# Attention in one core of Trainium2: six score tiles in one run, then all the values, with a marker read between the two key halves

## The chip, the cores and the metric

One core of one Trainium2 chip runs the whole program. The metric is the device time of one execution in microseconds (us), a median over runs. The core has five engines that work side by side, each through its own list of instructions in order: PE (TensorE, matrix multiplication; PEld is its weight load), DVE (VectorE), ACT (ScalarE), POOL (GpSimd) and SP (SyncE). POOL and SP here mostly issue DMA transfers. An engine that reaches an instruction whose input is not there waits, and everything behind it in its list waits too. Results of PE land in PSUM, which has eight banks per partition; one bank holds 512 numbers of 32 bits.

## The reference

Sigmoid attention over 8 batches, 12 heads, 448 positions and head size 64, then a feed-forward layer with an exact GELU. The program spends its first quarter in the attention and the rest in the feed-forward layer.

```python
# q, k, v: (8, 12, 448, 64); w_in: (768, 2048); w_out: (2048, 768)
scores = (1.0 / np.sqrt(64)) * np.matmul(q, k.transpose(0, 1, 3, 2)) - np.log(448)
attn = 1.0 / (1.0 + np.exp(-scores))
y = np.matmul(attn, v)
x = y.transpose(0, 2, 1, 3).reshape(8 * 448, 12 * 64)
h = x @ w_in
out = (0.5 * h * (1.0 + erf(h / np.sqrt(2)))) @ w_out
```

## The kernel before

**Units.** The attention works in 24 units. Unit u is one batch and two pairs of heads, p = 0 and 1, with two heads j = 0 and 1 in each pair. The 448 keys of a head are three full chunks of 128 (c = 0, 1, 2) and a tail of 64. Scores are computed with the keys as output rows and the 448 queries as columns.

**Scores.** `scores(u, p, c)` makes one score tile for a pair: two heads, so two banks. The head size is 64, so a matmul needs only half of the rows of PE's array: head j takes row half j, and the two heads run side by side (64 rows by 128 columns each, "64*128" in the profile). For accuracy each of q and k is split in a high and a low part (`split_qk`, tiles `hi` and `lo`, 128x896 each), and three products are added, so a tile is three pairs of matmuls. Unit 0 has plain operands of 32 bits. The tail of all four heads is one tile, `scores_tail(u)`, made from the raw q and k with quarters of the array ("64*64"). After each tile ACT makes the probabilities `a` with a sigmoid (L353).

**Values.** The products with v have an output of 64 rows. For units 1 to 21, `quarters(u, turn)` uses four quarters of the array at a time (both pairs, both heads, one half of a chunk's 128 keys). In turn 0 pair p takes key half p, in turn 1 the other. Both turns add into the same two banks, so turn 1 may not run beside turn 0. `values_tail(u)` adds the 64 tail keys the same way. Units 0, 22 and 23 ("plain") use `values` with all 128 rows instead.

**Order.** The order of each engine's instructions is the order of the code: it is written out by hand (`manual_schedule`), and a wait is put only where data or a buffer asks for it. In a pass u of the main loop PE does the first three score tiles of unit u, turn 0 and the tail values of unit u-1, the other three score tiles and the tail scores of unit u, and turn 1 of unit u-1. So the scores run one unit ahead of the values, and PE goes back and forth between 64*128 and 64*64 twice in a pass.

**The other engines in a pass.** ACT has seven sigmoids, for units 3 to 17 the high part of pair 0 of the next unit (L342), and two steps of the weight decoder (L132, L135). DVE copies the two finished banks of unit u-1 to the tile `x` (`park`, L452), runs the decoder's `start` (L121, L122, L125) and `end` (L141, L146), and makes the splits (L344, L345). The decoder turns 64-bit weights into 32-bit ones; its chunks 0 to 15 are 128x768, the rest 128x512. `decode(u, place)` takes so many of its steps (start, scale, end) at three places in a pass. POOL then stores `x` to `scr_x` (L455) and decoded weights to `scr_f`. There is one buffer for `x`, so the next `park` waits until the store has landed. SP loads q, k, v and the raw weights.

**PSUM.** Three buffers of two banks for score tiles (`ps_sc`), one bank each for pair 0 and pair 1 of the values (`ps_av`). The feed-forward layer takes all eight banks after the attention.

**The end.** The feed-forward layer starts with two operand tiles `xh0`, `xl0` that were loaded and split during units 16 to 20; the next two (`xl`, split on L288 and L289) are loaded by SP when the attention's memory is free.

Of the kernel before, what the change touches and what calls it, by code (L numbers as in the profile page):

```python
# [16 lines left out]
P = 128  # L17
# [4 lines left out]
def tile_sigmoid_attention_gelu_ffn(  # L22
# [34 lines left out]
    one = const.tile([P, 8], F32, name="one")[:, :1]  # L57
# [147 lines left out]
    STEPS = {B * NU - 2: (2, 1, 1), B * NU - 1: (3, 2, 2)}  # L205
# [98 lines left out]
    x0 = []  # L304

    def attention(at, ps_sc, ps_av):
# [3 lines left out]
        def load(u):  # L310
# [4 lines left out]
            for ps in (slice(0, 1), slice(1, 2)) if u == 0 else (slice(0, 2),):  # L315
                hps = slice(2 * n + ps.start, 2 * n + ps.stop)
                nc.sync.dma_start(raw[:, ps, 0], q[b, hps].rearrange("p r s -> r p s"))
                for j in range(2):
                    src = k[b, hps, rows(j), j].rearrange("p r s -> r p s")
                    queue = nc.scalar if j == 0 and u == 0 else nc.sync  # L320
                    queue.dma_start(raw[rows(j), ps, 1], src)
# [59 lines left out]
        def scores_tail(u):  # L381
# [3 lines left out]
            sc = ps_sc.tile([P, 2, 512], F32, tag="sc", name=f"sc{u}_t")[:, :, :S]  # L385
# [10 lines left out]
        def bank(u, p):  # L396
            if (u, p) not in pavs:
                pavs[u, p] = ps_av.tile([P, 512], F32, tag=f"pav{p}", name=f"pav{u}_{p}")
            return pavs[u, p][:, :S]

        def values(u, p, chunks=range(FULL)):
            if u < 0:
                return
            pav = bank(u, p)
            for c in chunks:
                a = probs.pop((u, p, c))
                for j in range(2):
                    nc.tensor.matmul(  # L408
                        pav[rows(j)],
                        vals[u][:, p, j, c],  # L410
                        a[:, j],
                        start=c == 0 and (p == 0 or u == total - 1),
                        stop=c == FULL - 1 and p == 1 and u < total - 1,
                    )

        def values_tail(u):
            if u < 0:
                return
            a = probs.pop((u, 0, FULL))
            for p, j in QUARTERS:  # L420
                nc.tensor.matmul(  # L421
                    bank(u, p)[rows(j)],
                    vals[u][rows(p), p, j, FULL],
                    a[rows(p), j],
# [482 lines left out]
```

## Time and profile before

| | us |
|---|---|
| median of 3 runs | 1033.49 (1033.11 to 1035.11) |
| the profiled execution, its own time | 1033.18 |
| its span in the trace | 1031.4 |
| first score matmul, in the chain that ended last | 5.11 |
| first matmul of the feed-forward layer, there | 250.46 |
| PE busy in the span | 1026.4 |
| DVE busy, ACT busy | 783.4, 605.2 |

The profiled execution took 1.8 us more than its span, which lies around the span. The rows below are from that one execution. In a row of the time line the columns are: start in us, length in us, engine, line of the code, operation, output<-input, shape, how many were merged, and in brackets how long the engine had been idle and what ended that. PE's matmuls overlap each other, so the distance between two starts says what one costs, not its length.

### The profile page before, as it was taken

To read this page: it belongs to the slowest core of one execution; us is meant where nothing else is said; L and a number is where in the kernel's file an instruction comes from. 1 tells how busy PE (TensorE), PEld (TensorE's weight loads), DVE (VectorE), ACT (ScalarE), POOL (GpSimd) and SP (SyncE) were. 2 spreads that over 40 slices of the span, in tenths; PEclk is the share of its full clock that TensorE was granted. 3 is DMA by queue.
4 is the path that set the end of the run, shared out by engine and by line. 5 is a ranking of instruction groups with operands and counts; after the bars stand their busy time and mean duration, and the time that the engine had idled before them with its cause. 6 is when DMAs were issued, how large, how long until landed. Compare 5 with 4: busy or idle time off the path is not lost.

```text
span 1031.4 us, 16513 instructions
## 1 busy us (share of the span) xinstructions
PE 1026.4 (100%) x6429; PEld 908.1 (88%) x6429; DVE 783.4 (76%) x989; ACT 605.2 (59%) x804; POOL 118.0 (11%) x186
## 2 busy tenths in 40 slices
PE   9999999999999999999999999999999999999998
PEld 5555555556999999999999999999999999999998
DVE  3676767795799688997678888566888875678875
ACT  6788787875445465455366645644665555466552
POOL 0111112001323362115000000100000000000000
PEclk9999999999999999999999999999999999999999
DMA  9999999995688798588644445734444553434441
GB/s 300 310 305 308 296 314 297 330 306 183 214 265 265 259 318 314 154 287 308 201 148 123 127 132 163 236 98 136 136 122 125 161 167 101 123 109 137 137 135 66
DMA packets 85933, 211.84 MB, mean 205 GB/s; under 512 B 9376, under 2 KB 35872, under 8 KB 85856
## 3 DMA queue, kind: packets, MB, share of 16 engines
q1 hardware_dynamic: 70672, 155.20, 50.2%
q0 software_dynamic: 14880, 55.26, 15.0%
q8 instruction: 50, 0.82, 0.3%
q10 hardware_dynamic: 304, 0.34, 0.1%
q14 instruction: 27, 0.22, 0.1%
HBM read 163.38 MB, written 50.33 MB: 207 GB/s over the span
## 4 chain that ended last, share of the span: by engine, by line
PE 100%; DVE 0%; DVEq 0%; issue 0%
PE pf L545 75%; PE pav L436 10%; PE sc L370 9%; PE sc_t L387 2%; PE pav L421 2%; PE pav L408 1%; PE warm L468 0%; DVE zero L464 0%; DVE tmp L582 0%; DVEq L903 0%; DVE one L465 0%
## 5 line engine op out<-in xcount | busy, mean ns | idle before, releaser
L545 PE MATMUL pf<-op,whl 128*128 128x448 f32 x2016 | 382.8, 353 | 0.0
L545 PEld LDWEIGHTS pf<-op,whl 128*128 128x128 f32 x2016 | 380.3, 189 | 1.8 <-DVE op L582 0.8
L253 ACT CAST whl<-wst 128x768 fp32r<-128x768 f32 x212 | 176.4, 833 | 241.5 <-PE pf L545 212.7
L545 PE MATMUL pf<-xh_p,whl 128*128 128x448 f32 x1008 | 273.4, 352 | 0.0
L260 DVE TENSOR_TENSOR whl<-wst,whl 128x768 fp32r<-128x768 f32 x212 | 201.8, 953 | 51.7 <-ACT whl L253 51.6
L545 PEld LDWEIGHTS pf<-xh_p,whl 128*128 128x128 f32 x1008 | 190.5, 189 | 0.2
L545 PE MATMUL pf<-xl_p,whl 128*128 128x448 f32 x504 | 177.6, 352 | 0.0
L353 ACT ACTIVATE a<-sc 128x896 f32<-128x896 f32 x144 | 121.2, 916 | 42.5 <-PE sc L370 42.5
L582 DVE TENSOR_TENSOR op<-g,op 128x896 fp32r<-128x896 f32 x112 | 121.4, 1085 | 1.4 <-ACT op L592 1.3
L592 ACT CAST op<-g 128x896 fp32r<-128x896 f32 x112 | 104.7, 935 | 2.6 <-PE pf L545 2.6
L545 PE MATMUL pf<-xh,whl 128*128 128x448 f32 x384 | 104.3, 353 | 0.0
L436 PE MATMUL pav<-a,v 64*64 64x448 f32 x1008 | 103.7, 540 | 0.0
L545 PEld LDWEIGHTS pf<-xl_p,whl 128*128 128x128 f32 x504 | 95.3, 189 | 0.0
L436 PEld LDWEIGHTS pav<-a,v 64*64 64x64 f32 x1008 | 36.7, 133 | 52.6 <-issue 47.6
L545 PEld LDWEIGHTS pf<-xh,whl 128*128 128x128 f32 x384 | 72.6, 189 | 0.7 <-issue 0.7
L582 DVE TENSOR_TENSOR g<-g,g 128x896 f32<-128x896 f32 x64 | 69.4, 1084 | 0.0
L452 DVE COPY x<-pav 128x448 f32<-128x448 f32 x48 | 27.9, 620 | 52.9 <-PE pav L436 44.2
L545 PE MATMUL pf<-xl,whl 128*128 128x448 f32 x192 | 67.7, 352 | 0.0
L579 ACT ACTIVATE g<-tmp 128x448 f32<-128x448 f32 x72 | 45.2, 627 | 36.1 <-DVE tmp L582 36.1
L582 DVE TENSOR_TENSOR tmp<-pf,g 128x448 f32<-128x448 f32 x72 | 44.9, 624 | 27.1 <-PE pf L545 26.6
L582 DVE TENSOR_TENSOR g<-pf,g 128x448 f32<-128x448 f32 x48 | 29.9, 624 | 33.8 <-PE pf L545 33.8
L370 PEld LDWEIGHTS sc<-lo,hi 64*128 64x128 f32 x276 | 26.0, 185 | 32.9 <-ACT a L353 18.1
(80 smaller groups left out, 975.1 us busy)
## 6 DMA issues: line engine op xcount, KB each, us to landing
wst<-scr_out SPq DMA_DIRECT2D x112, 384.0 KB, 3.2
wst<-scr_in SPq DMA_DIRECT2D x84, 384.0 KB, 3.1
v<-v_dram SPq DMA_DIRECT2D x24, 512.0 KB, 6.7
raw<-w_in_dram SPq DMA_DIRECT2D x16, 768.0 KB, 6.2
raw<-w_out_dram SPq DMA_DIRECT2D x24, 512.0 KB, 5.3
scr_x<-x POOLq DMA_DIRECT2D x24, 448.0 KB, 6.6
out_dram<-tmp SPq DMA_DIRECT2D x47, 224.0 KB, 2.2
qk<-q_dram SPq DMA_DIRECT2D x23, 448.0 KB, 6.1
```

The lines of the kernel that those rows point to most:

```text
L253: nc.scalar.copy(hl[:, 0], t)
L260: nc.vector.tensor_tensor(hl[:, 1], t, hl[:, 0], op=ALU.subtract)
L353: nc.scalar.activation(to, sc, AF.Sigmoid, bias=NEG_LOG_S, scale=SCALE)
L370: nc.tensor.matmul(sc[:, j], ks[rows(j), 1, keys], braid(qs[rows(j), 0]) if braided else qs[rows(j), 0], start=n == 0, stop=n == last,)
L387: nc.tensor.matmul(sc[rows(p), j], raw[rows(j), p, 1, FULL * P :], raw[rows(j), p, 0], start=True, stop=True,)
L421: nc.tensor.matmul(bank(u, p)[rows(j)], vals[u][rows(p), p, j, FULL], a[rows(p), j], start=plain(u) and u < total - 1 and p == 1, stop=u = ...
L436: nc.tensor.matmul(bank(u, p)[rows(j)], vals[u][rows(half), p, j, c], probs[u, p, c][rows(half), j], start=(turn, c) == (0, 0), stop=(turn ...
L452: nc.vector.tensor_copy(xs[u][:, p], bank(u, p))
L545: nc.tensor.matmul(bank, a, braid(m), **flags)
L579: nc.scalar.activation(straight(dst), unbraid(src), AF.Gelu)
L582: nc.vector.tensor_tensor(out, a, b, op=op)
L592: nc.scalar.copy(op[:, 0], src)
```

## The change

It touches the attention only.

- PSUM is one pool of four tags with two banks each. `place` deals them out: in a unit the six score tiles take buffers 0, 1, third, fourth, 0, 1, the values take the third and the tail scores of the next unit the fourth; third and fourth swap from unit to unit. Both pairs of the values are one tile `pav` of two banks.
- A unit is now done in one piece. PE makes all six score tiles of unit u, then all values of the same unit, in two half sets of quarter matmuls. The first set is the tail and one key half of chunks 0 to 2, the second the other key half. Between them stand the tail scores of unit u+1. So PE goes back and forth between the two shapes once in a unit.
- As the two half sets add into the same banks, DVE reads two columns of `pav` in between (L436 of the changed file, into `mark`). The first matmul of the second set waits for that read, and the read waits for the first set.
- The probabilities are used in the unit in which they are made. Chunk c of the first set waits for the sigmoids of both pairs' tiles c.
- DVE's work between `park` and the marker: the decoder's start and end, both splits of unit u+1. For next units 3 to 17 pair 1 is split first and pair 0, whose high part ACT makes, second. ACT makes that high part after all six sigmoids.
- Subtractions for `x0` and for the weight tiles (`W.low_to`), and the last decoder steps, stand behind the marker in `meanwhile`, ahead of `park`.
- Units 0 and 22 use quarters too; only unit 23 uses whole rows, in one piece. The number of decoder steps in the attention is the same.

```diff
+        def place(u, n, name):
+            third, fourth = (2, 3) if u % 2 == 0 else (3, 2)
+            i = (0, 1, third, fourth, 0, 1, third, fourth)[n]
+            return ps.tile([P, 2, 512], F32, tag=f"ps{i}", name=name)[:, :, :S]
...
-            sc = ps_sc.tile([P, 2, 512], F32, tag="sc", name=f"sc{u}_{p}_{c}")[:, :, :S]
+            sc = place(u, FULL * p + c, f"sc{u}_{p}_{c}")
...
-            sc = ps_sc.tile([P, 2, 512], F32, tag="sc", name=f"sc{u}_t")[:, :, :S]
+            sc = place(max(u - 1, 0), 2 * FULL + 1, f"sc{u}_t")
...
+        def values(u, meanwhile):
+            pav = pavs[u] = place(u, 2 * FULL, f"pav{u}")
+
+            def chunk(c, swap):
+                a = [probs[u, 0 if c == FULL else p, c] for p in range(2)]
+                for p, j in QUARTERS:
+                    half = rows(p ^ swap)
+                    nc.tensor.matmul(
+                        pav[rows(j), p],
+                        vals[u][half, p, j, c],
+                        a[p][half, j],
...
+            order = [0, 1, 2, FULL] if u == 0 else [FULL, 0, 1, 2]
...
+            for c in order:
+                chunk(c, 0)
+            nc.vector.tensor_copy(mark, pav[:, :, 0])
+            meanwhile()
+            scores_tail(u + 1)
             for c in range(FULL):
+                chunk(c, 1)
...
-        for u in range(total + 1):
+        for u in range(total):
+            for p in range(2):
+                for c in range(FULL):
+                    scores(u, p, c)
+            if u == 0:
+                scores_tail(u)
+            load(u + 3)
             decode(u, 0)
-            for c in range(FULL):
-                scores(u, 0, c)
-            if not plain(u - 1) and u > 0:
-                quarters(u - 1, 0)
-                values_tail(u - 1)
...
-            split_qk(u + 1, 0)
-            split_qk(u + 1, 1)
-            for c in range(FULL):
-                scores(u, 1, c)
-            scores_tail(u)
-            load(u + 3)
+            split_qk(u + 1, 1 if 2 < u + 1 <= LATE else 0)
+            if u > 0:
+                split_qk(u + 1, 0 if 2 < u + 1 <= LATE else 1)
+            decode(u, 1)
...
+            def meanwhile():
...
+                if u in (total - 5, total - 4):
+                    hi, lo = x0[u - total + 5]
+                    nc.vector.tensor_tensor(lo, lo.bitcast(F32), hi, op=ALU.subtract)
+                if u in (total - 3, total - 2):
+                    W.low_to(W.low + 2)
                 decode(u, 2)
-                park(u - 1, 1)
...
+            values(u, meanwhile)
+            for p in range(2):
+                park(u, p)
```

PE around the second half set, before: the tail scores of unit 3 (`sc3_t`) and then turn 1 of unit 2. In brackets stands what an instruction waits for.

```order
L370 MATMUL sc3_1_2_502<-hi3_1_359 128x448 x2
L387 MATMUL sc3_t_511<-qk3_197 64x448 [waits DMAHW7_49,DMAHW6_49,Activation_49]
L387 MATMUL sc3_t_511<-qk3_197 64x448 [waits DMAHW0_49]
L387 MATMUL sc3_t_511<-qk3_197 64x448 x2
L436 MATMUL pav2_0_458<-a2_0_0_317,v2_215 64x448
```

PE at the same place in the changed program: the end of the first half set of unit 3, the tail scores of unit 4, the second half set of unit 3.

```order
L409 MATMUL pav3_549<-a3_0_2_496,v3_354 64x448
L409 MATMUL pav3_549<-a3_1_2_523,v3_354 64x448 [waits Activation_49]
...
L393 MATMUL sc4_t_567<-qk4_301 64x448 [waits DMAHW6_49,DMAHW5_49,PE_49]
L393 MATMUL sc4_t_567<-qk4_301 64x448 [waits DMAHW7_49]
L393 MATMUL sc4_t_567<-qk4_301 64x448 x2
L409 MATMUL pav3_549<-a3_0_0_478,v3_354 64x448 [waits DVE_49]
```

The second set followed the tail scores without a wait of its own; now its first matmul waits for DVE.

DVE in one pass before, from one `park` to the last split (units 3 and 6 in the names, decoder chunks 2 and 3).

```order
L452 COPY x3_657<-pav3_0_579 128x448
L452 COPY x3_657<-pav3_1_581 128x448
L121 TENSOR_SCALAR me3_663<-raw3_429 128x768
L122 TENSOR_SCALAR me3_663<-raw3_429 128x768
L125 SCALAR_TENSOR_TENSOR me3_663<-raw3_429,me3_663 128x768
L141 SCALAR_TENSOR_TENSOR me2_542<-raw2_221,me2_542 128x768
L146 SCALAR_TENSOR_TENSOR wd2_668<-me2_542 128x768
L345 TENSOR_TENSOR lo6_0_719<-qk6_518,hi6_0_718 128x896
L344 CAST hi6_1_722<-qk6_518 128x896
L345 TENSOR_TENSOR lo6_1_723<-qk6_518,hi6_1_722 128x896
```

DVE in one unit of the changed program, from `park` to the marker.

```order
L447 COPY x3_586<-pav3_549 128x448 x2
L122 TENSOR_SCALAR me2_650<-raw2_245 128x768
L123 TENSOR_SCALAR me2_650<-raw2_245 128x768
L126 SCALAR_TENSOR_TENSOR me2_650<-raw2_245,me2_650 128x768
L142 SCALAR_TENSOR_TENSOR me1_529<-raw1_243,me1_529 128x768
L147 SCALAR_TENSOR_TENSOR wd1_655<-me1_529 128x768
L345 CAST hi5_1_660<-qk5_410 128x896
L346 TENSOR_TENSOR lo5_1_661<-qk5_410,hi5_1_660 128x896
L346 TENSOR_TENSOR lo5_0_665<-qk5_410,hi5_0_664 128x896
L436 COPY ones_63<-pav4_670 128x2
```

The instructions are the same but for the order of the two splits and the marker, which stands behind all of them.

ACT in one pass before, from the first sigmoid of unit 3 to the decoder's steps.

```order
L353 ACTIVATE a3_0_0_438<-sc3_0_0_431 128x896
L353 ACTIVATE a3_0_1_447<-sc3_0_1_440 128x896
L353 ACTIVATE a3_0_2_456<-sc3_0_2_449 128x896
L342 CAST hi4_0_476<-qk4_298 128x896
L353 ACTIVATE a3_1_0_491<-sc3_1_0_484 128x896
L353 ACTIVATE a3_1_1_500<-sc3_1_1_493 128x896
L353 ACTIVATE a3_1_2_509<-sc3_1_2_502 128x896
L353 ACTIVATE a3_0_3_516<-sc3_t_511 128x896
L132 ACTIVATE me1_421<-me1_421 128x768
```

ACT in one unit of the changed program.

```order
L354 ACTIVATE a3_0_0_478<-sc3_0_0_471 128x896
L354 ACTIVATE a3_0_1_487<-sc3_0_1_480 128x896
L354 ACTIVATE a3_0_2_496<-sc3_0_2_489 128x896
L354 ACTIVATE a3_1_0_505<-sc3_1_0_498 128x896
L354 ACTIVATE a3_1_1_514<-sc3_1_1_507 128x896
L354 ACTIVATE a3_1_2_523<-sc3_1_2_516 128x896
L343 CAST hi4_0_543<-qk4_301 128x896
L133 ACTIVATE me1_529<-me1_529 128x768
L136 ACTIVATE me1_529<-me1_529 128x768
L354 ACTIVATE a4_0_3_572<-sc4_t_567 128x896
```

The high part of the next unit moved from behind three sigmoids to behind six.

## Rows read from the trace of the kernel before

**Rows 1.** The page: PE's busy time, share and instructions, with the other engines; and the granted clock of TensorE in 40 slices of the span (9 is 90% or more).

```profile
PE 1026.4 (100%) x6429; PEld 908.1 (88%) x6429; DVE 783.4 (76%) x989; ACT 605.2 (59%) x804; POOL 118.0 (11%) x186
PEclk9999999999999999999999999999999999999999
```

**Rows 2.** Busy time by stretch, for 30 to 240 us: PE, PEld, DVE, ACT, POOL with instructions, granted clock, DMA share, GB/s.

```profile
30.00:240.00 210.00, 210.00 (x2060) 114.02 (x2054) 162.20 (x224) 169.94 (x209) 28.17 (x41) 1.00 0.97 300
```

**Rows 3.** The time line of one pass (the scores of unit 10): PE's matmuls, and two weight loads of turn 1.

```profile
102.53 0.46 PE L370 MATMUL sc<-lo,hi 64*128 64x448 f32 x2
102.82 0.35 PE L370 MATMUL sc<-hi,lo 64*128 64x448 f32 x2
...
104.15 0.35 PE L370 MATMUL sc<-hi 64*128 64x448 f32 x2
104.43 2.49 PE L436 MATMUL pav<-a,v 64*64 64x448 f32 x24
107.60 0.46 PE L370 MATMUL sc<-lo,hi 64*128 64x448 f32 x2
...
111.43 0.15 PEld L436 LDWEIGHTS pav<-a,v 64*64 64x64 f32 x4 [0.22 <-issue]
111.81 0.15 PEld L436 LDWEIGHTS pav<-a,v 64*64 64x64 f32 x4 [0.22 <-issue]
112.67 0.46 PE L370 MATMUL sc<-lo,hi 64*128 64x448 f32 x2
```

**Rows 4.** The time line of DVE from the end of that pass to the end of the next.

```profile
112.80 1.16 DVE L452 COPY x<-pav 128x448 f32<-128x448 f32 x2 [2.50 <-PE pav L436]
113.87 0.55 DVE L121 TENSOR_SCALAR me<-raw 128x768 uint32<-128x768 uint32 x1
114.34 0.55 DVE L122 TENSOR_SCALAR me<-raw 128x768 uint32<-128x768 uint32 x1
114.93 0.96 DVE L125 SCALAR_TENSOR_TENSOR me<-raw,me 128x768 uint32<-128x768 uint32 x1
115.80 0.96 DVE L141 SCALAR_TENSOR_TENSOR me<-raw,me 128x768 uint32<-128x768 uint32 x1
116.80 0.96 DVE L146 SCALAR_TENSOR_TENSOR wd<-me 128x768 f32<-128x768 uint32 x1
117.68 1.08 DVE L345 TENSOR_TENSOR lo<-qk,hi 128x896 fp32r<-128x896 f32 x1
118.68 0.62 DVE L344 CAST hi<-qk 128x896 fp32r<-128x896 f32 x1
119.33 1.09 DVE L345 TENSOR_TENSOR lo<-qk,hi 128x896 fp32r<-128x896 f32 x1
122.93 1.16 DVE L452 COPY x<-pav 128x448 f32<-128x448 f32 x2 [2.51 <-PE pav L436]
```

**Rows 5.** The time line of ACT in the same stretch: three sigmoids after scores that began at 107.60, three in a full queue, and the high part behind them.

```profile
108.47 2.54 ACT L353 ACTIVATE a<-sc 128x896 f32<-128x896 f32 x3 [1.54 <-PE sc L370]
...
113.72 2.52 ACT L353 ACTIVATE a<-sc 128x896 f32<-128x896 f32 x3
116.12 0.95 ACT L342 CAST hi<-qk 128x896 fp32r<-128x896 f32 x1
```

**Rows 6.** Three hand-overs from the time lines of DVE, PEld and ACT: the only `park` that waited for the store of `x`, the weight load that waited for it; then a cast on ACT and the subtraction on DVE that waits for it, at the start of the feed-forward layer.

```profile
204.98 1.16 DVE L452 COPY x<-pav 128x448 f32<-128x448 f32 x2 [2.42 <-DMA scr_x<-x]
206.19 0.20 PEld L436 LDWEIGHTS pav<-a,v 64*64 64x64 f32 x7 [0.22 <-DVE x L452]
255.61 1.31 ACT L288 CAST xh<-xl 128x1344 fp32r<-128x1344 f32 x1 [9.70 <-DMA xl<-scr_x]
256.96 1.56 DVE L289 TENSOR_TENSOR xl<-xl,xh 128x1344 fp32r<-128x1344 f32 x1 [5.29 <-ACT xh L288]
```

**Rows 7.** Groups by line and shape, 0 to 275 us: count, busy us, mean ns of one, idle before.

```profile
L345 DVE TENSOR_TENSOR lo<-qk,hi 128x896 fp32r<-128x896 f32 x46 | 50.1, 1090 | 1.1
L452 DVE COPY x<-pav 128x448 f32<-128x448 f32 x48 | 27.9, 620 | 52.9 <-PE pav L436 44.2 <-PE pav L421 6.3 <-DMA scr_x<-x 2.4
L125 DVE SCALAR_TENSOR_TENSOR me<-raw,me 128x512 uint32<-128x512 uint32 x9 | 6.3, 696 | 0.3
L121 DVE TENSOR_SCALAR me<-raw 128x512 uint32<-128x512 uint32 x9 | 3.8, 425 | 0.0
L465 DVE MEMSET one<- 128x1 f32 x1 | 0.1, 59 | 0.0
```

**Rows 8.** The store of `x`: the issue behind the `park` of 193.88 us on POOL, and the time from issue to landing of the stores from 60 to 215 us.

```profile
195.33 0.72 POOL L455 DMA_DIRECT2D scr_x<-x  x1 [6.31 <-DVE x L452]
...
DMA to landing us min/median/max: 5.9/7.0/9.6
```

**Rows 9.** The chain that ended last, in order of time (start, length, what): its beginning and its last piece; and DVE's first split.

```profile
1.39 3.73 PE warm L468 x9
5.11 4.73 PE sc L370 x24
9.84 0.91 PE sc_t L387 x8
...
250.46 777.29 PE pf L545 x4104
...
11.54 0.63 DVE L344 CAST hi<-qk 128x896 fp32r<-128x896 f32 x1 [10.19 <-DMA qk<-k_dram]
```

More of the change, by code (lines that the diff above doesn't have):

```diff
@@ L55, in tile_sigmoid_attention_gelu_ffn @@
     ctx.enter_context(tc.manual_schedule())
-    one = const.tile([P, 8], F32, name="one")[:, :1]
+    ones = const.tile([P, 8], F32, name="ones")
+    one, mark = ones[:, :1], ones[:, 2:4]
     WU = NC * P
@@ L314, in load @@
             raw = at.tile([P, 2, 2, S], F32, tag="qk", name=f"qk{u}", bufs=3)
-            for ps in (slice(0, 1), slice(1, 2)) if u == 0 else (slice(0, 2),):
-                hps = slice(2 * n + ps.start, 2 * n + ps.stop)
-                nc.sync.dma_start(raw[:, ps, 0], q[b, hps].rearrange("p r s -> r p s"))
+            for pp in (slice(0, 1), slice(1, 2)) if u == 0 else (slice(0, 2),):
+                hps = slice(2 * n + pp.start, 2 * n + pp.stop)
+                nc.sync.dma_start(raw[:, pp, 0], q[b, hps].rearrange("p r s -> r p s"))
                 for j in range(2):
@@ L320, in load @@
                     queue = nc.scalar if j == 0 and u == 0 else nc.sync
-                    queue.dma_start(raw[rows(j), ps, 1], src)
+                    queue.dma_start(raw[rows(j), pp, 1], src)
             raws[u] = raw
@@ L394, in scores_tail @@
             sigmoid(u, 0, FULL, sc, False)
[L396 to L402, printed above, removed]
-                return
[L404 to L424, printed above, removed]
-                    start=plain(u) and u < total - 1 and p == 1,
-                    stop=u == total - 1 or plain(u) and p == 0,
-                )
-        def plain(u):
-            return u in (0, total - 2, total - 1)
@@ L465, in attention @@
         nc.vector.memset(one, 1.0)
-        warm = ps_sc.tile([P, 2, 512], F32, tag="sc", name="warm")
-        for _ in range(9):
-            nc.tensor.matmul(
-                warm[:, 0, :S], zero[:, 0, :P], braid(zero[:, 0]), start=True, stop=True
-            )
+        warm = place(0, 0, "warm")
+        for i in range(9):
+            nc.tensor.matmul(warm[:, 0], zero[:, 0, :P], braid(zero[:, 0]), start=True, stop=True)
         load(0)
@@ L500, in attention @@
                 W.high_to(W.ready + 2)
[L501 to L525 removed]
+            def meanwhile():
+                if u == 0:
+                    split_qk(1, 1)
+                if u in (total - 5, total - 4):
[3 more added lines that the diff above has]
+                    W.low_to(W.low + 2)
+                decode(u, 2)
+            values(u, meanwhile)
+            for p in range(2):
+                park(u, p)
             load_v(u + 2)
@@ L868, in tile_sigmoid_attention_gelu_ffn @@
     with tc.tile_pool(name="at", bufs=1) as at:
-        with psum("ps_sc", 3) as ps_sc, psum("ps_av", 1) as ps_av:
-            attention(at, ps_sc, ps_av)
+        with psum("ps", 1) as ps:
+            attention(at, ps)
     late = ctx.enter_context(tc.tile_pool(name="late", bufs=1))
```

70 lines of the change are left out of this document (21 added, 49 removed).

## The prediction

> **What bounds the kernel now.** I read the page first. PE is busy 100% of the span at a granted clock of 9 tenths or more in every slice [rows 1]; the stretch from 30 to 240 us shows a clock of 1.00, which is the 2.4 GHz level, and PE busy for all of its 210 us, with DVE at 162 us and ACT at 170 us [rows 2]. The chain that ended last is PE from the first score to the last matmul: the attention runs from 5.11 to 250.46, so 245.35 us, and the feed-forward layer takes the remaining 777.29 us [rows 9]. The change leaves that layer's PE work alone, so the question is what the 245.35 us become.
>
> Then I read one pass closely. Scores start at 102.53 and again at 112.67: a pass takes 10.14 us [rows 3]. Nine pairs of score matmuls go at 0.19 us each (102.82 to 104.15 is seven of them), so 1.70 us, but from the first score to the first value matmul it takes 1.90 (102.53 to 104.43). Groups of four quarter matmuls go at 0.376 us (111.43 to 111.81), a pass has sixteen, 6.02 us. 18 x 0.189 + 6.02 = 9.42, so 0.72 us of a pass go with its two trips between the shapes, 0.36 us each. Nothing else holds PE up.
>
> DVE and ACT have slack. DVE works from 112.80 to 120.42, then idles 2.51 us until PE frees the next pair of banks at 122.93 [rows 4]. ACT waits 1.54 us for scores [rows 5]. What this slack is worth once PE waits for them within a unit decides the case.
>
> **Removed: one trip in each unit.** A unit without any wait would take 10.14 - 0.36 = 9.78 us. Laid out from its first score at t = 0: two stretches of nine pairs, the second without its start-up, put the first quarter group at 1.90 + 1.70 = 3.60. From 104.43 to 107.60 eight groups take 3.17 us [rows 3]; eight times 0.376 is 3.01, and the rest I read as 0.05 more for the first group behind a trip and 0.11 between the last group and the next shape. The first half set has eight groups, 3.60 to 6.66, the tail scores two, the second half set begins at 7.41 and ends at 9.67, and 0.11 later the next unit starts. For units 1 to 22, at best, this saves 22 x 0.36 = 7.9 us.
>
> **Added: chunks that wait for sigmoids.** ACT's first sigmoid starts 0.87 us after the first score (107.60 to 108.47), and in a full queue they follow each other every 0.80 us (113.72 to 116.12 is three) [rows 3, 5]. So sigmoid n starts at 0.87 + 0.80n and ends about 0.92 later. Chunks 0, 1 and 2 need sigmoids 3, 4 and 5, done at 4.2, 5.0 and 5.8; PE wants them at 4.4, 5.2 and 5.9. That fits to within 0.1 us, and delays only the end of the first set, which the marker's wait below covers. Buffers come free in time too: tiles 4 and 5 need sigmoids 0 and 1, the values need sigmoid 2, the tail scores sigmoid 3, and score tile 3 needs `park`, done at 1.3 where PE comes at 1.9.
>
> **Added: the marker.** It waits for three things.
> - PE: the first set is through by about 7.0.
> - DVE's own list. It starts 0.13 us after the next unit's first score (112.67 to 112.80). The starts in [rows 4] give the steps: park 1.07, decoder start 0.47 + 0.59 + 0.87, decoder end 1.00 + 0.88, cast 0.65, subtraction 1.00, subtraction 1.00. Sum 7.53, so the marker can start at 7.66. Before, this ran in PE's shadow with 2.5 us to spare; now it ends ahead of the wait.
> - ACT's high part of pair 0. It now stands behind six sigmoids: 0.87 + 4.80 = 5.67, and 0.95 for itself, 6.62; DVE starts 0.04 us after ACT ends (256.92 to 256.96) [rows 6]; the last subtraction takes 1.00. Marker at 7.66 again.
>
> Two chains that have nothing in common but the unit's start say 7.66. So even a lighter DVE list would not help while ACT makes the high part.
>
> The marker itself, a copy of two columns from PSUM, is not in the trace. DVE's subtraction of 896 columns takes 1.09 and that of 1344 takes 1.56, 1.04 ns a column [rows 6, 7]; the copy of 448 columns takes 0.62, which leaves 0.15 for everything but columns. The lower bound is the memset of one column, 0.06. The upper bound is 0.20, the fixed part with a third on top for a read that nothing overlaps, an estimate from the same row. I take 0.16, as the copy from PSUM is the nearest row. The Trainium skill says in "Perfetto Trace Analysis", section "Optimizing Scalar/DVE Operations", that DVE pays about 125 ns for an access to PSUM and that the profiled length is about twice that; the copy's row shows 0.15 and not 0.25, and by the page's figure the sum below would be 15 x 0.1 = 1.5 us higher.
>
> PE starts 0.05 us after DVE ends: the second copy of the `park` of 204.98 ends at 206.14 and the waiting load goes at 206.19 [rows 6]. So the second half set begins at 7.66 + 0.16 + 0.05 = 7.87 instead of 7.41, and its first group, not loaded ahead, costs 0.05 more. **PE waits 0.51 us, the unit takes 10.29 us,** 0.15 more than before. Bounds: marker 0.06 and no dearer first group give 10.14; marker 0.20, sigmoids at 0.81 (2.54 us for three, the last 0.92) and the subtraction's full length of 1.09 ahead of the marker give 10.46.
>
> **Units that differ.** Unit 0: scores to 9.84 as before, its tail and sixteen groups follow without a trip; DVE's first cast at 11.54 and its subtraction are done ahead of the marker [rows 9]. The next unit starts at 16.78: 11.67 us. Unit 1: no decoder, both casts on DVE, nothing late: 9.78. Units 2 to 16 go by the sum above (in unit 2 DVE's list is short, but ACT's chain holds): 15 x 10.29 = 154.35. Unit 17: both casts on DVE, 0.65 more in its list: 10.94. Unit 18: decoder start on 128x512, where L125 takes 0.70 for 0.96 and L121 0.43 for 0.55 [rows 4, 7], so 0.53 less: 10.41. Units 19 to 22: the decoder end shrinks as well, 0.54; marker at 7.24, nearly hidden: 9.85 each, 39.40. Unit 23: six score tiles, 3.60, two groups, twelve groups of whole rows, two small gaps: 9.17.
>
> Three small waits. The store of `x` may land behind the next `park`: it is issued 1.45 us after `park` starts (193.88 to 195.33) and takes 5.9 to 9.6 us [rows 8]; units 19 to 22 leave 9.85 - 1.45 = 8.4, so I add 0.3. In unit 22 two subtractions and a decoder start stand between marker and `park`, 3.1 us where 2.4 fit; score tile 3 of unit 23 gets its bank late: 0.24. At the end SP issues the load of `xl` behind two raw loads that wait for DVE, some 1.6 us later than before; its last use had 1.9 us to spare: 0.2, with up to 3 if the raw loads land late.
>
> **The sum.** 11.67 + 9.78 + 154.35 + 10.94 + 10.41 + 39.40 + 9.17 + 0.74 = 246.46 against 245.35: 1.1 us more. The profiled execution would go from a span of 1031.4 to 1032.5 and from 1033.18 to 1034.3; the median of the runs shown is 0.31 above it, so from 1033.49 to **1034.6 us**. With the bounds of the unit on fifteen of them (-2.3 and +2.6), 17 and 18 along with them, this is 1032 to 1037.5. What is saved on trips (8 us and the one stall of 0.4 at 204.98) is given back as a wait for the marker.
>
> **The rivals.**
> - *The marker hides behind the tail scores.* Then a unit takes 9.80 and the attention loses 15 x 0.49 + 1.1 + 0.6 more: 1025.5 us. It needs both chains 0.46 us shorter than rows 4 and 5 say. For it: only the marker itself is new. Against: every step of both chains stands in a row, and the steps before it are the same instructions. Chance 0.09.
> - *The store of `x` ends last* (slower). Its landing decides above about 8.8 us in a unit of 10.3. Before, the one late store cost DVE 2.42 us [rows 6] and PE only 0.4; now a late `park` moves DVE's list, the marker and PE by its full length, and the bank of score tile 3 as well. With the DMA share at 0.97 [rows 2] landings of 9.6 in five units cost 0.8 each, 4 us: 1038.6, more if more are late. For it: 9.6 was seen. Against: the median is 7.0. Chance 0.20, and the late load of `xl` belongs here.
> - *The clock falls as PE idles half a microsecond in each unit.* Before, every slice is granted in full, the one with the stall at 204.98 too [rows 1]. The nine warm-up matmuls took 3.73 us, 0.41 each against 0.19 later [rows 9], so a unit at that pace would lose some 11 us and the kernel pass 1200. The Trainium skill describes such a fall for a PE that idles often between groups ("TensorE: Matmul & The Clock Gate", "A second HAM failure mode: psum-queue depth-cycling"); no row here shows one. Chance 0.02.
> - The forecast: 0.69.
>
> **How the numbers follow.** A measurement of this kernel can tell about 0.2%, 2.1 us, from no change: 1031.4 and 1035.6 are the borders. Of the forecast's 0.69, I put 0.02 below, 0.52 between and 0.15 above. With the hidden marker, faster has 0.11; with the late stores and the clock, slower has 0.37; same has 0.52. The range of 1031.0 to 1038.6 leaves out the hidden marker and the worse half of the late stores with the clock, 0.09 and 0.11.
>
> **What would show it.** In the profile after: score starts every 10.2 to 10.4 us in units 2 to 16, about 10.9 in unit 17, 9.8 to 9.9 from unit 19; PE's weight loads of the second half set waiting about half a microsecond for DVE's two-column copy; that copy starting right behind the last subtraction, 7.6 to 7.8 us after the unit's first score; ACT's cast of the high part ending 0.04 us ahead of that subtraction or a little earlier. Idle time of DVE ahead of the marker that PE ends would show the chains to be shorter than I have them, and a second half set without wait would make the prediction wrong by the full 8 us. DVE waiting for the store of `x` in several units would show the second rival.

## The result and the profile after

The changed kernel takes 1041.22 us (median of 6 runs, 1040.13 to 1041.81); the kernel before, beside it, 1033.62. The ratio is 1.0067, with a 95% interval of 1.0054 to 1.0081: slower by 7.6 us. The forecast was 1034.6 with a range of 1031.0 to 1038.6.

The profiled execution took 1041.77 us with a span of 1040.0; the forecast for the span was 1032.5. Its page shows the busy line, as in [rows 1], and the shares of the engines in the chain that ended last:

```profile
span 1040.0 us, 16662 instructions
PE 1024.8 (99%) x6477; PEld 918.8 (88%) x6477; DVE 784.6 (75%) x1012; ACT 603.5 (58%) x804; POOL 117.8 (11%) x186
PE 91%; DMA 3%; DVE 3%; ACT 1%; issue 1%; SPq 0%; DVEq 0%; ACTq 0%
```

Before, PE alone made up the chain from the first score on. Now 9% of it lies elsewhere: PE waits for the others. Where, the waits from 5 to 256 us say (who waits, for whom, us in total, times, longest):

```profile
PEld pav L409 <- DVE ones L436: 23.1, 23, 1.9
PE pav L409 <- DVE ones L436: 6.7, 18, 1.1
DVE x L447 <- DMA scr_x<-x: 2.7, 1, 2.7
ACT whl L254 <- DMA wst<-scr_f: 1.8, 2, 1.5
```

The marker shows as `ones` (its two columns lie in that tile). PE itself idles for it in 18 units, 6.7 us in all; the rest of the weight loads' 23.1 us is hidden behind the tail scores. The store of `x` was late once. The wait at the layer's start, 3.3 us, lies behind this stretch and follows below.

**A unit in the steady state**, from the time lines of PE, DVE and ACT (columns as in [rows 3 to 5]; unit 9 starts at 100.80):

```profile
104.40 3.27 PE L409 MATMUL pav<-a,v 64*64 64x448 f32 x32
107.46 0.96 PE L393 MATMUL sc_t<-qk 64*64 64x448 f32 x8
108.71 2.49 PE L409 MATMUL pav<-a,v 64*64 64x448 f32 x24 [0.28 <-DVE ones L436]
111.12 0.46 PE L376 MATMUL sc<-lo,hi 64*128 64x448 f32 x2
```

```profile
100.94 1.15 DVE L447 COPY x<-pav 128x448 f32<-128x448 f32 x2 [2.61 <-PE pav L409]
...
106.46 2.13 DVE L346 TENSOR_TENSOR lo<-qk,hi 128x896 fp32r<-128x896 f32 x2
108.50 0.15 DVE L436 COPY ones<-pav 128x2 f32<-128x2 f32 x1
```

```profile
101.68 4.96 ACT L354 ACTIVATE a<-sc 128x896 f32<-128x896 f32 x6 [2.12 <-PE sc L376]
106.47 0.98 ACT L343 CAST hi<-qk 128x896 fp32r<-128x896 f32 x1
```

DVE works from 100.94 to 108.65 with no idle stretch (the lines left out are the decoder and the cast of the first split). The marker starts 7.70 us after the unit's first score (forecast 7.66) and takes 0.15; the second half set starts 0.06 later, and the unit takes 10.32 (forecast 10.29). PE's idle time of 0.28 counts from the modelled end of the tail scores. At 0.376 for a group of four, their two groups from 107.46 would have let the second set begin at 108.21; it began at 108.71, so the delay is 0.50. ACT's high part ends at 107.45, just as DVE comes to the subtraction that needs it (the second of the two from 106.46): both chains do end together.

**The end of the attention and the start of the feed-forward layer**, time lines of DVE and PE:

```profile
251.83 0.70 DVE L142 SCALAR_TENSOR_TENSOR me<-raw,me 128x512 uint32<-128x512 uint32 x1 [2.69 <-ACT me L136]
...
255.41 0.69 DVE L147 SCALAR_TENSOR_TENSOR wd<-me 128x512 f32<-128x512 uint32 x1
256.02 1.15 DVE L447 COPY x<-pav 128x448 f32<-128x448 f32 x2
```

```profile
249.73 4.30 PE L424 MATMUL pav<-a,v 128*64 128x448 f32 x22
257.32 0.43 PE L517 MATMUL pf<-xh,whl 128*128 128x448 f32 x1 [3.28 <-DVE x L447]
...
257.77 0.54 PE L517 MATMUL pf<-xh,whl 128*128 128x448 f32 x2
...
259.24 0.95 PE L517 MATMUL pf<-xh,whl 128*128 128x448 f32 x2
```

The layer's first matmul waits 3.28 us for `park` of unit 23, which stands on DVE behind the last decoder steps, and those wait for ACT. Then the matmuls go at about half pace: 0.95 for two at 259.24, where it was 0.54 at 257.77. The busy times by stretch (columns as in [rows 2]) tell why; the granted clock stands behind POOL's busy time:

```profile
30.00:240.00 210.00, 204.15 (x2040) 119.08 (x2037) 158.37 (x234) 166.58 (x207) 28.21 (x41) 1.00 0.94 298
...
254.00:257.30 3.30, 0.04 (x2) 0.01 (x1) 3.10 (x6) 0.49 (x2) 0.00 (x0) 1.00 0.55 192
257.30:260.00 2.70, 2.68 (x11) 2.55 (x12) 0.00 (x0) 0.00 (x0) 2.21 (x3) 0.73 0.80 248
260.00:263.00 3.00, 3.00 (x12) 2.82 (x11) 0.00 (x0) 0.00 (x0) 0.00 (x0) 0.67 0.93 298
263.00:266.00 3.00, 3.00 (x18) 3.00 (x17) 1.07 (x1) 1.75 (x2) 0.00 (x0) 1.00 0.95 359
```

From 30 to 240 us, in 210 us with a wait in nearly every unit, the grant is 1.00. In the two stretches behind the idle one, 5.7 us together, it is 0.73 and 0.67, so partly the level of 1.2 GHz and partly that of 2.4, and only then full again. What is missing there from the full grant, 0.27 of 2.70 us and 0.33 of 3.00, makes 1.72 us. The layer takes 779.01 us in the chain, 777.29 before: the same 1.72 more. The mean granted clock of a whole execution is 0.997 or 0.998 in four of the six runs of the change and 1.000 in the other two (1040.13 and 1040.82 us), so the clock does not fall in every execution.

**All pieces against the forecast** (profiled execution, us):

| piece | forecast | measured | difference |
|---|---|---|---|
| first score | 5.11 | 5.17 | +0.06 |
| unit 0 | 11.67 | 13.49 | +1.82 |
| unit 1 | 9.78 | 9.81 | +0.03 |
| units 2 to 16 | 154.35 | 154.91 | +0.56 |
| units 17 and 18 | 21.35 | 21.54 | +0.19 |
| units 19 to 22, with 0.3 and 0.24 | 39.94 | 39.87 | -0.07 |
| unit 23 up to the layer, with 0.2 | 9.37 | 12.53 | +3.16 |
| feed-forward layer | 777.29 | 779.01 | +1.72 |

These add up to 7.5 us, the whole difference between the forecast span (1032.5) and the measured one (1040.0). Three pieces out of eight carry 6.7 of it, and none of the three is a steady unit.

### The profile page after: what moved, and what is told of

Its sections match the earlier page's. It is cut to its first block, busy times and chain, and to the rows that moved or that the text cites. A ratio compares the mean times of both kernels' runs of the same rounds, so it can differ in the third digit from the quotient of the medians.

```text
span 1040.0 us, 16662 instructions
## 1 busy us (share of the span) xinstructions
PE 1024.8 (99%) x6477; PEld 918.8 (88%) x6477; DVE 784.6 (75%) x1012; ACT 603.5 (58%) x804; POOL 117.8 (11%) x186
## 4 chain that ended last, share of the span: by engine, by line
PE 91%; DMA 3%; DVE 3%; ACT 1%; issue 1%; SPq 0%; DVEq 0%; ACTq 0%
PE pf L517 75%; PE pav L409 9%; PE sc L376 5%; DMA scr_x<-x 2%; DMA qk<-k_dram 1%; ACT a L354 1%; PE sc_t L393 1%; DVE x L447 1%; DVE lo L346 1%; DMA wst<-scr_f 1%; DVE me L142 0%; DVE hi L345 0%; DVE ones L436 0%; DVE me L126 0%; DVE me L122 0%
## 5 line engine op out<-in xcount | busy, mean ns | idle before, releaser
L409 PE MATMUL pav<-a,v 64*64 64x448 f32 x1296 | 133.4, 545 | 6.7 <-DVE ones L436 6.7
L409 PEld LDWEIGHTS pav<-a,v 64*64 64x64 f32 x1296 | 50.2, 132 | 77.3 <-issue 36.4
L346 DVE TENSOR_TENSOR lo<-qk,hi 128x896 fp32r<-128x896 f32 x46 | 49.4, 1092 | 2.8 <-ACT hi L343 1.7
```

Of the source, the lines that this page charges most:

```text
L346: nc.vector.tensor_tensor(lo, raw, hi, op=ALU.subtract)
L409: nc.tensor.matmul(pav[rows(j), p], vals[u][half, p, j, c], a[p][half, j], start=not swap and c == order[0], stop=c == (order[-1], FULL - ...
```

## The experiments

My theory after the result: (1) in the steady units the two chains that end at the marker cost half a microsecond each; (2) unit 23 is late because the layer's first bank belongs to one PSUM pool, which is free only when `park` has read its last bank; (3) the idle stretch brings down the clock; (4) unit 0 waited for a load that landed late in this execution. Medians below are in us, with those of the kernel before from the same chip. The lengths are from each profile, for the units 2 to 16 the usual length of one; the last two columns are the start and the length of the feed-forward layer.

| kernel | median | before | ratio (95%) | units 2 to 16 | layer starts | layer |
|---|---|---|---|---|---|---|
| the change | 1041.22 | 1033.62 | 1.0067 (1.0054 to 1.0081) | 10.32 | 257.32 | 779.0 |
| marker one step earlier | 1031.83 | 1034.00 | 0.998 (0.9972 to 0.9989) | 9.81 | 246.38 | 779.0 |
| decoder end behind the marker | 1040.07 | 1034.00 | 1.0057 (1.0045 to 1.0069) | 10.32 | 255.98 | 779.0 |
| `park` of unit 23 first | 1039.01 | 1034.00 | 1.0046 (1.0034 to 1.0058) | 10.33 | 253.31 | 779.6 |
| two pools | 1036.57 | 1034.00 | 1.0029 (1.0018 to 1.0040) | 10.32 | 252.78 | 777.6 |
| weight loads early | 1040.59 | 1033.86 | 1.0066 (1.0053 to 1.0079) | 10.32 | 255.10 | 780.2 |
| all mends | 1028.68 | 1033.86 | 0.995 (0.9937 to 0.9962) | 9.81 | 242.59 | 779.4 |
| all mends, tail scores early | 1040.04 | 1033.86 | 1.0057 (1.0044 to 1.0070) | 10.29 | 254.43 | 780.1 |
| all mends, short tail | 1026.30 | 1033.97 | 0.9927 (0.9914 to 0.9941) | 9.81 | 242.07 | 777.4 |

**The marker one step earlier.**

```diff
-            nc.vector.tensor_tensor(lo, raw, hi, op=ALU.subtract)
+            rest.append(lambda: nc.vector.tensor_tensor(lo, raw, hi, op=ALU.subtract))
+            if hold: held_lo.extend(rest)
...
             nc.vector.tensor_copy(mark, pav[:, :, 0])
+            for work in held_lo: work()
```

> The marker stands one step earlier in DVE's list: the last subtraction of the next unit's splits (in units 1 and 17 on, the cast and subtraction of the second split) is done behind it. My theory: in units 2 to 16 two chains of 7.7 us, DVE's list and ACT's high part with the subtraction behind it, end at the marker and PE waits about half a microsecond for that. Without that last step DVE's list ends at 6.6 to 6.7, the marker waits for PE alone at about 7.1, and PE finds it done at 7.41. Units 2 to 16 fall from 10.32 to 9.8 to 9.9, unit 17 from 11.12 to about 9.9, unit 18 from 10.42 to 9.9: some 9 us in all, the time to about 1032. Rival A, the marker itself holds PE up (PE must run dry, be read and start again, whatever stood ahead of it): units stay above 10.2 and the time at 1039 or more. Rival B, the subtraction behind the marker makes the next park or the next high part late: score starts move from the marker's wait to a wait of the third score tile, units near 10.1.

Every unit from 1 to 21 took 9.81. The time lines of DVE and PE in the second half of a unit:

```profile
102.21 0.16 DVE L444 COPY ones<-pav 128x2 f32<-128x2 f32 x1 [0.16 <-PE pav L417]
102.28 1.08 DVE L349 TENSOR_TENSOR lo<-qk,hi 128x896 fp32r<-128x896 f32 x1
```

```profile
101.93 0.97 PE L401 MATMUL sc_t<-qk 64*64 64x448 f32 x8
102.69 2.47 PE L417 MATMUL pav<-a,v 64*64 64x448 f32 x24
105.09 0.46 PE L384 MATMUL sc<-lo,hi 64*128 64x448 f32 x2
```

Now the marker waits for PE, not PE for the marker: it is done at 102.37, and PE comes to the second half set at 102.69, 0.76 after the tail scores began, without a wait. One subtraction of 1.09 us on the wrong side of the marker (in unit 1 and from unit 17 on with its cast) cost 9 us. Rivals A and B fall: the marker costs PE nothing when its inputs are there, and in units 1 to 21 nothing behind it came late. Two stalls are left at the end, and the first is rival B after all: 1.32 us ahead of score tile 3, the fourth, of unit 23 (the `park` of unit 22 stands behind two weight subtractions, as my term of 0.24 had it, and now also behind the cast and the subtraction that this edit moved there), and still 2.58 us at the layer's start.

**The decoder's end behind the marker.**

```diff
-                dec.go(STEPS.get(u, (2 if u > BEGIN else 1, 1, 0))[place])
+                dec.go(STEPS.get(u, (1, 0, 2 if u > BEGIN else 1))[place])
```

> The decoder's end (L142, L147, 1.9 us on DVE in units 3 to 17) stands behind the marker; ACT's high part of pair 0 stays behind the six sigmoids. My theory, as in the prediction: two chains of equal length end at the marker. DVE's own list falls from 7.66 to 5.8, but the last subtraction must wait for ACT's high part, which ends 6.65 after the unit's first score, and takes 1.06: marker at 7.7 as before, units 3 to 16 stay at 10.25 to 10.35 (unit 17, both casts on DVE and so no wait for ACT, falls from 11.12 to about 9.9), the time at about 1040. DVE then shows about 1 us idle ended by ACT's cast in each unit. Rival: DVE's list alone decides, ACT's cast is only just early enough and would start earlier: units at 9.8 to 9.9, time 1033 to 1034.

DVE's list is 1.9 us lighter ahead of the marker, and units 2 to 16 stay at 10.32, while unit 17, whose splits need nothing of ACT, falls from 11.12 to 9.81. DVE's time line shows what holds it:

```profile
103.73 1.09 DVE L346 TENSOR_TENSOR lo<-qk,hi 128x896 fp32r<-128x896 f32 x1
106.63 1.09 DVE L346 TENSOR_TENSOR lo<-qk,hi 128x896 fp32r<-128x896 f32 x1 [1.80 <-ACT hi L343]
107.64 0.15 DVE L436 COPY ones<-pav 128x2 f32<-128x2 f32 x1
```

There are 1.80 us of idle time (I had expected about 1), ended by ACT: the second chain is as long as the first. Relieving one of two equal chains gives nothing, as the prediction had it; the early marker takes off the step that both share. Units 17 to 21 are 2.1 us shorter together, but unit 22 takes 11.83 instead of 10.23, which gives most of it back: its third score tile waits 1.67 us for ACT, whose tail sigmoid stands behind the weight casts that the run with early weight loads, below, is about.

**`park` of unit 23 ahead of the decoder steps; two pools.**

```diff
-                decode(u, 2)
+                if u < total - 1: decode(u, 2)
...
             for p in range(2):
                 park(u, p)
+            if u == total - 1: decode(u, 2)
```

> Only unit 23 differs: the two copies of its values to x stand ahead of the last four decoder steps on DVE, not behind them. My theory: the first matmul of the feed-forward layer waits for these copies (3.28 us at 257.32) and the four steps ahead of them are what makes them late. Then the layer starts about 3 us earlier, at some 254.2 to 254.5; and as PE is not idle, the clock is granted in full at the layer's start (0.67 to 0.73 for some 6 us in the changed kernel) and the layer takes 777.3 instead of 779.0: together 4.5 to 5 us, about 1036.4. Rival: the layer's first operands (the load of xl, or the first weight tiles) are what comes last a little behind, then it starts at 256 or later and at most 1.5 us are gained; or the layer's 1.7 us do not come from the clock after the idle stretch and stay: then 1038.

```diff
-            return ps.tile([P, 2, 512], F32, tag=f"ps{i}", name=name)[:, :, :S]
+            return ps[i == 3].tile([P, 2, 512], F32, tag=f"ps{i}", name=name)[:, :, :S]
...
-        with psum("ps", 1) as ps:
+        with psum("ps", 1) as ps_a, psum("ps_b", 1) as ps_b:
```

> The four pairs of banks come from two pools, three pairs from one and the fourth from the other, as the kernel before had two pools; the copies of unit 23 stay late. My theory: the first matmul of the feed-forward layer waits for the copies only because its bank belongs to the one pool that is given back as a whole, behind the last reader of any of its banks. With two pools its first bank is free when PE's own values are through, and the layer starts at about 254.2 without an idle stretch; the clock stays. About 1036.4, like the run with the copies first. Rival: the layer would have stalled anyway a few matmuls on, when it comes to the banks that the copies still hold or to xl: then PE idles 1 to 3 us later in the layer's first microseconds, and the gain is under 2 us, 1039 to 1041.

PE with `park` first, and then PE and DVE with two pools:

```profile
253.31 0.43 PE L520 MATMUL pf<-xh,whl 128*128 128x448 f32 x1 [1.35 <-DVE x L447]
...
267.32 0.46 PE L520 MATMUL pf<-xh,whl 128*128 128x448 f32 x1 [0.15 <-ACT xh L289]
268.91 0.46 PE L520 MATMUL pf<-xl,whl 128*128 128x448 f32 x1 [1.14 <-DVE xl L290]
```

```profile
248.12 4.73 PE L424 MATMUL pav<-a,v 128*64 128x448 f32 x24
252.78 0.46 PE L517 MATMUL pf<-xh,whl 128*128 128x448 f32 x1
...
254.85 1.15 DVE L447 COPY x<-pav 128x448 f32<-128x448 f32 x2
```

With two pools, the layer starts as the values end, although `park` is as late in its unit as in the change and begins 2.07 us into the layer. So it is the pool that makes the first matmul wait, not a bank that it needs. (No row names a bank. That the values of unit 23 lie in the fourth pair in both kernels, and the layer's first tile among the six other banks, is read from the code.) The time fell to 1036.57 (expected 1036.4), unit 23 to 9.18, and the layer to 777.6. With `park` first, 1.35 us of the wait stay, since two copies, 1.15 us together, now stand bare behind PE's last value, and the rival was partly right: the decoder steps moved behind `park` hold back the load of `xl` (in SP's waits the raw loads ahead of it wait 17.6 us for DVE's L142), and PE waits 0.15 and 1.14 us for it later. The time is 1039.01, where I expected 1036.4.

The clock can be settled too, by the stretches at the start of the layer with `park` first and in the next experiment (weight loads early, where the idle stretch stays):

```profile
253.30:256.00 2.70, 2.69 (x14) 2.70 (x15) 2.60 (x5) 0.00 (x0) 2.21 (x3) 1.00 0.42 58
```

```profile
252.00:255.10 3.10, 0.00 (x0) 0.03 (x1) 2.92 (x5) 0.26 (x2) 0.00 (x0) 0.84 0.62 180
255.10:258.00 2.90, 2.90 (x8) 2.64 (x9) 0.00 (x0) 0.00 (x0) 2.21 (x3) 0.50 0.92 305
258.00:261.00 3.00, 3.00 (x10) 2.70 (x9) 0.00 (x0) 1.27 (x1) 0.00 (x0) 0.51 0.92 304
```

After 1.35 us of idle time the grant stays 1.00; in the idle stretch of 3.12 it falls (0.84), and behind it it is 0.50 and 0.51, the 1.2 GHz level, for 5.9 us, and the layer takes 780.2. With the early marker, where the idle stretch is 2.58, the grant is 0.73 and 0.68 (over 2.7 and 3.0 us) and the layer takes 779.0; with the decoder's end late (3.29 us) 0.67 and 0.76 (over 3.0 us each), and 779.0. The sum that gave 1.72 for the change gives 2.92, 1.69 and 1.71 here, and these three layers took 2.9, 1.7 and 1.7 us more than the 777.29 of the kernel before. So the clock is all that the idle stretch costs the layer.

**The weight loads early.**

```diff
+            if u == total - 4:
+                W.load_to(4)
```

> Only the issue of two weight loads differs: they go out in unit 20, not when ACT's cast in unit 21 asks for them. My theory: in the changed kernel ACT's cast of the weight tiles waits 1.49 and 0.32 us for these loads, stands ahead of the tail sigmoid, and so holds PE up by some 0.35 us in unit 22. With the loads early ACT does not wait for them, and unit 22 falls from 10.23 to 9.85 to 9.95; the time falls by about 0.3 us, too little to see in it. Rival: unit 22 is held by its late copies of the values (two subtractions of 0.9 stand ahead of them), and stays at 10.1 to 10.2.

In the change, ACT's time line in unit 22 reads (the tail sigmoid is the last line, and the third score tile waits for it until 236.03):

```profile
233.18 0.83 ACT L254 CAST whl<-wst 128x768 fp32r<-128x768 f32 x1 [1.49 <-DMA wst<-scr_f]
234.33 0.83 ACT L254 CAST whl<-wst 128x768 fp32r<-128x768 f32 x1 [0.32 <-DMA wst<-scr_f]
235.07 0.91 ACT L354 ACTIVATE a<-sc_t 128x896 f32<-128x896 f32 x1
```

With the loads early ACT does not wait there, and unit 22 takes 9.88 instead of 10.23. So that unit was held by its weight loads, not by the late copies that I had put 0.24 on. The time does not show so little.

**All mends.** The early marker, in unit 0 too; two pools; the weight loads early; the two weight subtractions of unit 22 behind its `park`.

```diff
-            split_qk(u + 1, 1 if 2 < u + 1 <= LATE else 0)
+            split_qk(u + 1, 1 if 2 < u + 1 <= LATE else 0, u == 0)
...
-                if u in (total - 3, total - 2):
+                if u == total - 3:
                     W.low_to(W.low + 2)
...
                 park(u, p)
+            if u == total - 2:
+                W.low_to(W.low + 2)
```

> The marker early in every unit, unit 0 too (there ahead of both splits of unit 1), two pools of banks, the weight loads of unit 22 issued two units earlier, and the two weight subtractions of unit 22 behind its copies of the values. My theory, by the terms that the earlier runs showed one by one: unit 0 at 11.6, units 1 to 21 at 9.81, unit 22 at 9.8 to 9.95 (no wait of the tail sigmoid for the weight loads), unit 23 at 9.2 without a wait of its third score tile for the copies, the feed-forward layer 777.3 to 777.6 without an idle stretch ahead and with the clock granted in full: the layer starts at 241.5 to 242.2, the time is 1024 to 1027, 7 to 9 us below the kernel before. Rival: PE, without its waits, runs into a transfer that was hidden (the next store of x, the raw q and k, the load of xl), and 2 us or more of this stay away: 1028 or more.

The time is 1028.68, 5.2 us below the kernel before. Units 2 to 21 came as expected (unit 0 took 12.10 for 11.6, unit 1 9.95), but the time lies 1.7 us above the range I had given, and the rival came true with the load of `xl`: the layer took 779.4 for 777.3 to 777.6. PE waits once, and SP's time line shows the loads behind it:

```profile
259.87 0.46 PE L532 MATMUL pf<-xl,whl 128*128 128x448 f32 x1 [1.14 <-DVE xl L290]
```

```profile
246.56 2.16 SPq L286 DMA_DIRECT2D xl<-scr_x  x4
```

**All mends, with the tail scores ahead of the first set's last chunk.**

```diff
             for c in order:
+                if u > 0 and c == order[-1]:
+                    scores_tail(u + 1)
                 chunk(c, 0)
...
-            scores_tail(u + 1)
+            if u == 0:
+                scores_tail(u + 1)
```

> As the run with all mends, but in units 1 to 22 the tail scores of the next unit stand ahead of the first set's last chunk, so nothing of PE lies between the two half sets and the wait for the marker is bare. My theory: the tail scores are what hides the marker's way (PE's last result, 0.16 for the marker, the way back). In the run with the early marker that way took 0.45 to 0.5 us from the last result of the first set and the tail scores 0.75. Bare, a unit takes 9.81 plus 0.4 to 0.5, 10.2 to 10.3, and the kernel 9 to 11 us more than the run with all mends. Rival: without DVE's backlog the two half sets follow each other nearly unheld (the marker's way under 0.2 us), then at most 4 us more.

Units 2 to 19 go from 9.81 to 10.29, and the kernel from 1028.68 to 1040.04. PE and DVE between the half sets:

```profile
106.98 0.93 PE L417 MATMUL pav<-a,v 64*64 64x448 f32 x8
108.19 2.49 PE L417 MATMUL pav<-a,v 64*64 64x448 f32 x24 [0.28 <-DVE ones L446]
```

```profile
107.98 0.16 DVE L446 COPY ones<-pav 128x2 f32<-128x2 f32 x1 [0.91 <-PE pav L417]
```

Two groups of 0.376 end the first set at 107.73; 0.25 later DVE starts, 0.16 for the marker, 0.05 back to PE: the bare way takes 0.46. So the tail scores (0.75) are what makes the marker free, and 0.3 us is the slack that other work ahead of it may use up.

**All mends, with a short tail.**

```diff
-    STEPS = {B * NU - 2: (2, 1, 1), B * NU - 1: (3, 0, 4)}
+    STEPS = {B * NU - 2: (2, 1, 1), B * NU - 1: (3, 0, 1)}
```

> As the run with all mends, but unit 23 takes only one of its last four decoder steps; the other three go to the feed-forward layer, whose pace makes up for them. In the run with all mends the layer waited 1.14 us for the second xl, 17.3 us into it, and SP issued the loads of xl at 246.56, right behind the last decoder end on DVE, 4 us after PE had finished the attention (242.59). My theory: the four steps hold these loads back, through SP's load of raw weights ahead of them. With one step they go out at about 243 to 243.5, both parts are ready by about 256, PE does not wait for them, and the layer takes 777.3 to 777.8 instead of 779.4: 1.2 to 2 us less, 1026.5 to 1027.5. Rival: the three steps moved into the layer make something there late (a mixed weight tile, a cast ahead of a gelu), or the loads land no earlier since the raw loads go beside them: no gain, 1028 to 1030.

SP's load of `xl` and the chain that ended last:

```profile
242.23 2.25 SPq L286 DMA_DIRECT2D xl<-scr_x  x4
```

```profile
242.14 777.36 PE pf L532 x4104
```

The loads go out at 242.23 instead of 246.56, PE shows no idle stretch from the first score to its last matmul, and the time is 1026.30, ratio 0.9927 (0.9914 to 0.9941): 7.7 us below the kernel before, near the 7.9 that 22 trips of 0.36 were worth at best.

**The kernel before, twice.**

> The kernel before, unchanged, to see its first microseconds once more. In the changed kernel's profile DVE's first cast of unit 1 waits for its load until 14.37, in the profile of before until 11.54. My theory: the landing differs from execution to execution (11.94 to 13.56 in the four runs since), the order of the loads is the same; here it falls between 11.4 and 14.4, and PE does not wait for the cast as long as it is done by about 16. Rival: the changed order delays the load, then this run shows 11.5 again, within 0.1.

> The kernel before, unchanged, for a third look at its first microseconds. DVE's first cast of unit 1 came at 11.53 and 11.54 in two profiles of it; with the changed order it came between 11.94 and 14.37 in six. If the landing differs from execution to execution in both kernels alike, this one should lie above 11.6; if it is 11.5 once more, the changed kernels load later by a cause that the order of the loads does not show.

The two executions took 1033.9 and 1034.91. The first time DVE's first cast of unit 1 came at 11.53, as in [rows 9], and it looked as if the change delayed the load. The second time it came at 14.22, and PE, in the kernel before, waited for it (DVE, then PE):

```profile
14.22 0.63 DVE L344 CAST hi<-qk 128x896 fp32r<-128x896 f32 x1 [12.88 <-DMA qk<-k_dram]
```

```profile
16.12 0.46 PE L370 MATMUL sc<-lo,hi 64*128 64x448 f32 x2 [0.98 <-DVE lo L345]
```

So the landing differs from execution to execution in both kernels. In profiles with the changed order in unit 0 the cast came at 11.94, 11.95, 12.24, 12.46, 13.56 and 14.37, and unit 0 took 11.64, 11.64, 11.63, 11.94, 12.95 and 13.49. Whether the change also makes the load later on average, three profiles of the kernel before are too few to tell.

## Why the prediction was wrong

The steady units, on which most of its working was spent, came out as worked out: the trip saved (9.81 for 9.78 in unit 1), both chains at 7.70 for 7.66, the marker at 0.15 for 0.16, the unit at 10.32 for 10.29, units 18 and 19 to 21 at 10.42 and 9.88 for 10.41 and 9.85. Only unit 17 is further off, 11.12 for 10.94. So was the answer to the question where the gain goes: into a wait for the marker. The sentence of the Trainium skill that was weighed there ("Perfetto Trace Analysis", "Optimizing Scalar/DVE Operations"), by which the marker would take an estimated 0.25, does not hold here: the rows show 0.15 and 0.16.

**The step that failed is unit 23 up to the layer's first matmul**, "9.17" and the small wait of 0.2 behind it: 12.53 measured. It priced PE's own work and the loads of `xl`, but not what the first matmul of the layer waits for: that wait stood at nothing, and it was 3.28 us. Before, the layer started at 250.46 without a wait for `park`, and I carried that over. The change makes PSUM one pool, and so the layer's first bank waits for the last reader of all eight; and it moves the last decoder steps ahead of that reader on DVE. I had described both edits and put a price on neither. The run with two pools undid the first alone and gave back the whole wait.

**The layer itself** was taken over at 777.29, with the argument that the change leaves its PE work alone. The idle stretch ahead of it brought the clock down, which cost 1.72 us in the profiled execution; without the stretch, and with `xl` in time, the layer takes 777.4 to 777.6. As a rival, I had asked whether waits of half a microsecond in each unit would bring the clock down. They do not: the grant is 1.00 from 30 to 240 us. It fell behind the one long stretch at the end, and by their mean clocks in four of the six executions only.

**Unit 0** was taken from one execution's landing at 11.54. This one landed at 14.37 and cost 1.82. The profile of the kernel before with a landing at 14.22 lost 0.98 itself, so of the difference between two profiles this is the part that says least about the change; how much of it is in the median of six runs the runs do not tell.

**Unit 22** got the right size by chance: 0.3 and 0.24 stood for a store and a late `park`, and what came was a wait of ACT for weight loads that the change issues later, 0.35. `W.low_to` also issues the next two loads; the change moved them with it (228.43 on SP, 215.06 before), and I had counted its subtractions only.

Of the rivals, the store of `x` ended last once (DVE idled 2.70 us for it, where it is 2.61 behind PE, in unit 3, which took 10.39), and once in the run with two pools (2.94 us, again in unit 3, which took 10.65), and not as a mechanism. The marker that hides came true only after its list was cut.

## What to carry to other kernels

When a change merges pools, ask of the first user of the space behind them what it waits for now: with one pool that is the last reader of any of its buffers, and a handful of cheap steps ahead of that reader became 3.3 us and, through the clock, 1.7 more. When a new wait is put into a steady loop, only what it needs should stand ahead of it on the engine that serves it: here one subtraction of 1.09 us, moved behind the marker, turned 7.6 us lost into 2.2 won, and work that lies between (0.75 us of tail scores) hides a way of 0.46. And price the start and the end of a loop from what each engine has queued there, as one would a steady pass: units 1 to 16 were right to 0.04 us each but for unit 3, with its late store, and the error was at the seams.

## What the runs showed of the hardware

- TensorE's granted clock fell in or just behind single idle stretches of 2.58, 3.12, 3.28 and 3.29 us, to 0.50 to 0.76 in the 5.7 to 6 us behind them, and stayed at 1.00 after one of 1.35. The feed-forward layer was 1.7 to 2.9 us longer for it than 777.3. The same length does not always give the same fall: 3.12 gave 0.50 and 0.51, 3.28 gave 0.73 and 0.67, and two of six executions of the change show a mean clock of 1.000.
- From the end of PE's last group of matmuls into two banks, past a read of two columns by DVE, to the first matmul that waits for that read: 0.46 us, of which the read takes 0.16.
- The load of the second unit's q and k, issued at the same place of SP's queue, was usable at 11.5 to 14.4 us in different executions.
